# Talking-heads attention: the mixing stage laid out in 64x64 and 64x32 array tiles, with the attention turned by VectorE

## The chip, the cores and the metric

The kernel runs on one core of a Trainium2 chip. The metric is the device time of one execution in microseconds (us), as the median of several runs. A profile is one further execution, recorded by the hardware profiler. The engines are called PE (TensorE's matmuls), PEld (its weight loads), DVE (VectorE), ACT (ScalarE), POOL (GpSimd) and SP (SyncE, here only a queue that issues DMAs).

## What is computed

Two blocks follow each other. All data are fp32; the two feed-forward weights come in as 64-bit floats. With B = 8 batches, 12 heads, S = 448 positions and head size 64:

```python
scores = scale * q @ k.transpose            # (B, 12, S, S)
scores = einsum('bhij,hg->bgij', scores, w_pre)
attn = exp(scores - max(scores, axis=-1))
attn = attn / (sum(attn, axis=-1) + 1e-09)
attn = einsum('bhij,hg->bgij', attn, w_post)
x = (attn @ v)                              # to (B, S, 768)

u = x + real(fft(fft(x, axis=1), axis=2))
un = (u - mean(u)) / sqrt(var(u) + 1e-06)
out = u + maximum(un @ w_ch1, 0) @ w_ch2    # 768 -> 3072 -> 768
```

The heads are mixed with each other before the softmax (`w_pre`) and after it (`w_post`). That mixing runs over the head index at every pair of positions, so neither of the two products has a long inner dimension.

## The kernel before

`mix_phase` computes the attention, the Fourier mixing and the conversion of the feed-forward weights to fp32. `ffn_phase` then normalizes and runs the two products with the weights (matmuls L660 and L700). The change touches `mix_phase` alone.

**Tiles.** A tile is ten rows of queries of one batch with all 12 heads, so 120 partitions: `R = 10`, `KR = 120`, 45 tiles a batch, 360 in all. Twelve tiles make a group of up to 120 rows, four groups a batch. For each pair of heads q and k are loaded, transposed by PE against an identity (L221) and multiplied (`emit_qk`, L233): the two heads of a pair stand in partitions 0 to 63 and 64 to 127, so each of the two matmuls uses 64 rows of the array and 120 columns. The scores go from PSUM to the SBUF tile `Sb` (by ACT, L104, or by DVE, L106). A DMA gathers ten rows of twelve heads into `Kr`, with 120 partitions (`emit_gather`, L247).

**Per tile** there is one chain of steps:

1. `emit_premix` (L253): a block-diagonal 120x120 matrix of `w_pre` mixes the heads, 448 columns, into PSUM tile `mx` (two buffers).
2. `emit_max` (L260, DVE): the maximum of each row, negated, in `nmx`.
3. `emit_exp` (L269, ACT): the exponential into `PP` (four buffers), with the row sums in `den`.
4. `emit_scale` (L277, L279 on DVE, L282 on POOL): the reciprocal of the sum is multiplied into a copy of the `w_post` matrix, `kw2s`.
5. `emit_flip` (L290): four matmuls that take `PP` as weights, 112 columns at a time, so that the second mixing comes out already transposed in `fl`.
6. `emit_pav` (L104 or L106): `fl` is copied to `Pav`.

**Per group**, `emit_av` (L314) multiplies `Pav` with v, 48 matmuls of 64 columns twice, and POOL folds the result for the Fourier transform (L327 to L331). **Per batch**, `emit_z` (L344, seven chunks) and `emit_s2` (L368, one call per group) make the two Fourier products; DVE adds them to the rows (L376, L379).

**Weights.** `emit_convert` runs 96 times: POOL issues a load of 384 KB of 64-bit words (L396) into one of two buffers `raw`, DVE makes fp32 of it in seven instructions (L407 to L420) on `tmp` and `top`, and SP stores it (L422).

**Order.** A loop over tiles writes the steps of tiles s-1 to s+6 one after another and inserts the other work from one list, `fill`, sorted by due times. A scheduler then sets the order on every engine, PE included. `_Evac` chooses ACT or DVE for each copy out of PSUM by a running estimate of both engines' load.

## Time and profile before

| | us |
|---|---|
| median of 3 runs | 3179.82 (3176.68 to 3180.89) |
| the profiled execution | 3191.58, span of the core 3189.8 |
| `mix_phase`, to the first transpose of `ffn_phase` | 0 to 1591.5 |
| PE busy over the span | 3019.4 (95%) |
| PEld / DVE / ACT / POOL busy | 2167.1 / 1162.7 / 792.9 / 519.8 |
| granted TensorE clock, mean | 0.963 |

A profile's page begins with the busy time of each engine. A row of digits gives busy tenths of 40 equal slices of the span, here about 80 us each. `PEclk` is the share of full speed that TensorE was granted in each slice. A view by stage repeats these sums for chosen stretches, with the number of instructions in brackets. A row of the view by line gives line, engine, operation, output<-inputs, shapes and count, then the busy time, the mean of one in ns, and the engine's idle time just before, with what ended it. A shape such as 64*120 on a matmul is rows times columns of the array that it uses. An fp32 matmul shows as two weight loads and two matmul instructions. The length of a matmul instruction includes the time its last result needs to come out, so neighbours overlap. The chain of waits follows the work that ended last back in time and counts each moment once.

### The profile page before, as it was taken

To read this page: it belongs to the slowest core of one execution; us is meant where nothing else is said; L and a number is where in the kernel's file an instruction comes from. 1 tells how busy PE (TensorE), PEld (TensorE's weight loads), DVE (VectorE), ACT (ScalarE), POOL (GpSimd) and SP (SyncE) were. 2 spreads that over 40 slices of the span, in tenths; PEclk is the share of its full clock that TensorE was granted. 3 is DMA by queue.
4 is the path that set the end of the run, shared out by engine and by line. 5 is a ranking of instruction groups with operands and counts; after the bars stand their busy time and mean duration, and the time that the engine had idled before them with its cause. 6 is when DMAs were issued, how large, how long until landed. Compare 5 with 4: busy or idle time off the path is not lost.

```text
span 3189.8 us, 39781 instructions
## 1 busy us (share of the span) xinstructions
PE 3019.4 (95%) x14768; PEld 2167.1 (68%) x14768; DVE 1162.7 (36%) x2911; ACT 792.9 (25%) x1940; POOL 519.8 (16%) x869
## 2 busy tenths in 40 slices
PE   6888888899999999999999999999999999999998
PEld 3665565676767776766787686686686786776875
DVE  4667777533333333333653032122121221221220
ACT  3333333354545354544110010010010010110100
POOL 4242242141313131211110100100100100000000
PEclk8788988899999999999899999999999999999999
DMA  7566666453444444444875444444444444444433
GB/s 194 140 156 165 169 178 164 120 113 66 107 73 104 80 100 89 84 81 91 267 251 176 163 159 158 162 153 158 175 139 168 171 154 147 166 168 148 154 111 109
DMA packets 179798, 457.07 MB, mean 143 GB/s; under 512 B 19743, under 2 KB 122655, under 8 KB 167063
## 3 DMA queue, kind: packets, MB, share of 16 engines
q1 hardware_dynamic: 155063, 361.71, 40.2%
q0 software_dynamic: 24544, 92.82, 9.9%
q8 instruction: 119, 1.95, 0.2%
q14 instruction: 72, 0.59, 0.1%
HBM read 317.60 MB, written 59.77 MB: 118 GB/s over the span
## 4 chain that ended last, share of the span: by engine, by line
PE 66%; DMA 14%; issue 12%; DVE 5%; POOL 2%; SPq 1%; ACT 0%; POOLq 0%; DVEq 0%; ACTq 0%
PE ms L314 9%; PE psP L660 8%; PE fl L290 8%; PE psP L700 8%; PE mx L253 7%; DMA raw<-in_moe_w_ch_dram 6%; PE psR L700 6%; PE psR L660 5%; PE ms L233 4%; PE ms L368 4%; PE psQ L700 3%; DMA w1t<-w1f 3%; PE ms L344 2%; PE psQ L660 2%; DMA out_dram<-u 1%
## 5 line engine op out<-in xcount | busy, mean ns | idle before, releaser
L660 PE MATMUL psP<-ub,w1t 128*128 128x256 f32 x2016 | 465.8, 384 | 30.8 <-DVE mv L619 16.7
L290 PEld LDWEIGHTS fl<-kw2s,PP 120*112 120x112 f32 (+1 forms) x2880 | 349.5, 185 | 210.9 <-issue 117.2
L660 PEld LDWEIGHTS psP<-ub,w1t 128*128 128x128 f32 x2016 | 383.7, 192 | 98.0 <-DMA w1t<-w1f 25.8
L700 PE MATMUL psP<-w2t,h 128*128 128x384 f32 x1344 | 436.9, 486 | 0.0
L290 PE MATMUL fl<-kw2s,PP 120*112 120x120 f32 (+1 forms) x2880 | 389.7, 281 | 44.1 <-POOL kw2s L282 25.6
L253 PE MATMUL mx<-Kr,kw 120*120 120x448 f32 x720 | 350.2, 570 | 33.4 <-ACT PP L269 26.3
L700 PEld LDWEIGHTS psP<-w2t,h 128*128 128x128 f32 x1344 | 254.8, 190 | 173.1
L314 PEld LDWEIGHTS ms<-vn,Pav 112*120 112x120 f32 (+1 forms) x3072 | 341.0, 195 | 20.9 <-issue 16.9
L314 PE MATMUL ms<-vn,Pav 112*120 112x64 f32 (+1 forms) x3072 | 340.2, 278 | 7.6 <-issue 6.7
L269 ACT ACTIVATE PP<-mx,nmx 120x448 f32<-120x448 f32 x360 | 228.2, 634 | 470.7 <-DVE nmx L260 430.8
L260 DVE TENSOR_REDUCE nmx<-mx 120x1 f32<-120x448 f32 x360 | 222.3, 618 | 256.4 <-PE mx L253 254.3
L282 POOL TENSOR_SCALAR kw2s<-kw2g,rcp 120x120 f32<-120x120 f32 x360 | 148.2, 412 | 716.8 <-DVE rcp L279 648.2
L104 ACT COPY Pav<-fl 112x480 f32<-112x480 f32 x310 | 177.1, 571 | 273.0 <-PE ms L314 141.2
L660 PE MATMUL psR<-ub,w1t 128*128 128x256 f32 x1008 | 232.7, 380 | 0.9 <-DMA w1t<-w1s 0.7
L700 PE MATMUL psR<-w2t,h 128*128 128x384 f32 x672 | 220.0, 486 | 0.0
L637 POOL TENSOR_TENSOR ub<-ub 128x768 f32<-128x768 f32 x28 | 50.5, 1825 | 1038.2 <-ACT ub L632 1037.7
L233 PE MATMUL ms<-kT,qT 64*120 64x448 f32 (+1 forms) x768 | 206.9, 609 | 6.7 <-DVE Sb L106 5.0
L660 PEld LDWEIGHTS psR<-ub,w1t 128*128 128x128 f32 x1008 | 191.3, 190 | 28.2 <-DMA w1t<-w1s 2.6
L700 PEld LDWEIGHTS psR<-w2t,h 128*128 128x128 f32 x672 | 126.4, 190 | 84.1
L104 ACT COPY Sb<-ms 120x448 f32<-120x448 f32 (+1 forms) x324 | 161.2, 531 | 48.9 <-PE ms L233 48.7
L709 DVE TENSOR_TENSOR u<-u,psP 128x384 f32<-128x384 f32 x56 | 31.1, 555 | 341.6 <-PE psP L700 341.6
L632 ACT COPY ub<-psQ 128x384 f32<-128x384 f32 x56 | 24.8, 481 | 481.0 <-PE psQ L630 481.0
(86 smaller groups left out, 2758.4 us busy)
## 6 DMA issues: line engine op xcount, KB each, us to landing
Kr<-Sb SPq DMA_DIRECT2D x352, 210.0 KB
w2t<-w2s SPq DMA_DIRECT2D x56, 1152.0 KB
w2t<-w2f SPq DMA_DIRECT2D x42, 1152.0 KB
w1t<-w1s SPq DMA_DIRECT2D x72, 576.0 KB
raw<-in_moe_w_ch_dram POOLq DMA_DIRECT2D x96, 384.0 KB, 5.8
w1t<-w1f SPq DMA_DIRECT2D x84, 384.0 KB
w1t<-w1f SPq DMA_DIRECT2D x96, 192.0 KB
w1t<-w1s SPq DMA_DIRECT2D x72, 192.0 KB
```

The costliest lines, as they stand in the source:

```text
L104: self.nc.scalar.copy(out=out, in_=in_)
L233: nc.tensor.matmul(sp[:n, :S], st["qT", hp][x * D:(x + 1) * D, g["i0"]:g["i0"] + n], st["kT", hp][x * D:(x + 1) * D, :], start=True, stop= ...
L253: nc.tensor.matmul(mx[:m, :S], kw1[:m, :m], tiles[T]["Kr"][:m, :], start=True, stop=True)
L260: nc.vector.tensor_reduce(nmx[:m, :], tiles[T]["mx"][:m, :S], axis=AX.X, op=ALU.max, negate=True)
L269: nc.scalar.activation(PP[:m, :], tiles[T]["mx"][:m, :S], ACTF.Exp, bias=tiles[T]["nmx"][:m, :], accum_out=den[:m, :])
L282: nc.gpsimd.tensor_scalar(kw2s[:m, :], kw2g[:m, :], rcp[:m, :], 1.0, op0=ALU.mult, op1=ALU.mult)
L290: nc.tensor.matmul(fl[:PC, jc * KR:(jc + 1) * KR], tiles[T]["PP"][:m, jc * PC:(jc + 1) * PC], tiles[T]["kw2s"][:m, :], start=True, stop=True)
L314: nc.tensor.matmul(ps[:n, hl * D:(hl + 1) * D], g["Pav"][:, jc * NH + h, :n], st["v", h // 2][:, h % 2, jc * D:(jc + 1) * D], start=(jc == ...
L344: nc.tensor.matmul(ps[:w, :SH + 1], g["xf"][par][:n, d0:d0 + w], ts[:n, g["gi"], par, :], start=(g["gi"] == 0), stop=(g["gi"] == NG - 1))
L368: nc.tensor.matmul(ps[:n, :DH + 1], st["z", par, ch][:, i0:i0 + n], tab[:w, ch, :], start=(ch == 0), stop=(ch == len(chunks) - 1))
L660: nc.tensor.matmul(p, w[m][:, i, kc, :], ub[:, i, kc, :], start=opens and kc == 0, stop=kc == NK - 1, skip_group_check=True)
L700: nc.tensor.matmul(p, lhs[i][:, half * NQ + kf, x * P:(x + 1) * P], w[:, kf, :], start=opens and half == 0 and kf == 0, stop=half == 1 and ...
```

## The change

The mixing stage gets another layout. The names of the steps mostly stay.

- **Steps of 20 rows.** `R = 5` rows times 12 heads are 60 partitions. Four such sets make a step: two in partition halves, two in the free dimension (`x` and `z`). A block of 56 rows is three steps, a group of 112 rows six; a batch is 24 steps, all are 192. Some rows are computed twice.
- **Tiles of the array.** `emit_qk`, `emit_premix` and `emit_av` issue matmuls of 64 rows and 64 (or 60) columns, four places in the array; `emit_postmix`, which takes the place of `emit_flip`, issues 64x32, eight places. The transposes and the Fourier products keep the full array.
- **Second mixing.** `PP` is now the moving operand. POOL scales `PP` itself by the reciprocal (twice 448 columns). The result `po` is not transposed by the matmul; DVE turns it in 32x32 blocks (`emit_turn`) into `Pv`, which takes the place of the copies to `Pav`.
- **Attention times v** has v as weights (64x64) and 120 columns of `Pv` moving, 84 matmuls a group. Its result is transposed, so `emit_x` turns it back with six PE transposes per group.
- **Buffers.** `mx` and `po` have two PSUM banks and one buffer each, `PP` two buffers, `Kr` three; `ms` keeps four banks.
- **Gathers.** Four DMAs of 60 partitions per step.
- **Order.** Other work stands in three lists, by the form of array it uses ("tile", "full", "none"). PE keeps the order in which the code is written; the other engines are still ordered by the scheduler. Conversions are due every 1.9 steps instead of every 3.5 tiles.

The core of the diff:

```diff
-R = 10
-KR = NH * R
-GT = 12
+R = 5
+KR = R * NH
+NB = 56
+BS = 3
+GT = 2 * BS
+GR = 2 * NB
-WSTEP = 3.5
+WSTEP = 1.9
...
-        ca, cd = 190.0 + n * 0.833, 70.0 + n * 1.042
+        ca, cd = 165.0 + n * 0.833, 150.0 + n * 1.042
...
-    pkr = pool("pkr", 6)
-    ppp = pool("ppp", 4)
+    pkr = pool("pkr", 3)
+    ppp = pool("ppp", 2)
+    ppv = pool("ppv", 2)
-    pmx = pool("pmx", 2, space=bass.MemoryType.PSUM)
-    pfl = pool("pfl", 2, space=bass.MemoryType.PSUM)
+    pmx = pool("pmx", space=bass.MemoryType.PSUM)
+    ppo = pool("ppo", space=bass.MemoryType.PSUM)
...
+    def emit_qk(n, xx):
+        for y in range(2):
+            lo = r0 + MG * y
+            for x in range(2):
+                nc.tensor.matmul(
+                    pss[x][64 * y:64 * y + r0 + 64 - lo, :S],
+                    st["qT", xx][64 * x:64 * x + 64, y, lo:r0 + 64],
+                    st["kT", xx][64 * x:64 * x + 64, y, :],
+                    start=True, stop=True)
...
+    def emit_gather(T):
+        for z in range(2):
+            for x in range(2):
+                nc.sync.dma_start(out=Kr[64 * x:64 * x + KR, z, :], in_=...)
...
+    def emit_premix(T):
+        mx = pmx.tile([P, 2, 512], F32, name="mx", tag="mx")
+        for x in range(2):
+            for z in range(2):
+                nc.tensor.matmul(mx[64 * z:64 * z + 64, x, :S],
+                                 kw1[64 * x:64 * x + KR, :],
+                                 Kr[64 * x:64 * x + KR, z, :], start=True, stop=True)
...
+    def emit_exp(T):
+        for x in range(2):
+            nc.scalar.activation(PP[:, x, :], steps[T]["mx"][:, x, :S], ACTF.Exp, ...)
...
+    def emit_scale(T):
+        nc.gpsimd.tensor_scalar(den[:, :], den[:, :], 1e-9, None, op0=ALU.add)
+        nc.vector.reciprocal(out=rcp[:, :], in_=den[:, :])
+        for x in range(2):
+            nc.gpsimd.tensor_scalar(PP[:, x, :], PP[:, x, :], rcp[:, x:x + 1], 1.0,
+                                    op0=ALU.mult, op1=ALU.mult)
+
+    def emit_postmix(T):
+        for y in range(2):
+            for c in range(2):
+                for z in range(2):
+                    o = 64 * y + 32 * c
+                    nc.tensor.matmul(po[o:o + 32, z, :S],
+                                     kw2[64 * z:64 * z + KR, y, :],
+                                     PP[64 * z:64 * z + KR, :, c * HS:(c + 1) * HS],
+                                     start=True, stop=True)
+
+    def emit_turn(T):
+        nc.vector.transpose(
+            g["Pv"][:, T % GT, :].rearrange("p (z s) -> p z s", z=2),
+            steps[T]["po"][:, :, :S])
+
+    def emit_av(g):
+        for pr in range(3):
+            for jb in range(C7):
+                for x in range(2):
+                    for y in range(2):
+                        i = 2 * pr + x
+                        nc.tensor.matmul(
+                            pss[y][64 * x:64 * x + 64, pr * nu * R:(pr + 1) * nu * R],
+                            st["v"][64 * y:64 * y + 64, i, jb * D:(jb + 1) * D],
+                            _ap(Pv, ...), start=(jb == 0), stop=(jb == C7 - 1))
...
+    with tc.manual_schedule(engines={mybir.EngineType.PE}):
+        while s < TOT or any(fill.values()):
+            held = []
+            take("none", s)
+            if 0 <= s + LM < TOT:
+                emit_premix(s + LM)
+                emit_max(s + LM)
+                emit_exp(s + LM)
+            take("tile", s)
+            if 0 <= s < TOT:
+                emit_postmix(s)
+                emit_turn(s)
+            if 0 <= s + LM < TOT:
+                emit_scale(s + LM)
+            if 0 <= s + LG < TOT:
+                emit_gather(s + LG)
+            take("full", s)
+            for fn in held:
+                fn()
+            s += 1
```

On PE, in the middle of a batch, the order before was this (L290 second mixing, L253 first mixing, L233 scores, L314 attention times v; a row is a matmul, `x4` four of them):

```order
L314 MATMUL ms<-vn,Pav 120x64 x48
L290 MATMUL fl<-kw2s,PP 112x120 x4
L253 MATMUL mx<-Kr,kw_122 120x448
L233 MATMUL ms<-kT,qT 120x448 x2
L290 MATMUL fl<-kw2s,PP 112x120 x4
L253 MATMUL mx<-Kr,kw_122 120x448
```

The same place now (L294 first mixing, L268 scores, L361 attention times v, L333 second mixing, L394 transposes of `emit_x`):

```order
L294 MATMUL mx<-Kr,kw_131 64x448 x4
L268 MATMUL ms<-kT,qT 64x448 x2
L268 MATMUL ms<-kT,qT 60x448 x2
L361 MATMUL ms<-Pv,vv 64x120 x84
L333 MATMUL po<-PP,kw_132 32x448 x8
L294 MATMUL mx<-Kr,kw_131 64x448 x4
L268 MATMUL ms<-kT,qT 64x448 x2
L268 MATMUL ms<-kT,qT 60x448 x2
L333 MATMUL po<-PP,kw_132 32x448 x8
L394 MATMUL ms<-ident,XT 112x128 x6
```

Scores now stand in every step, attention times v stands between the first mixing of one step and the second mixing of the step two before, and full-array work stands behind the second mixing.

On ACT, in the second half of the stage, the order before mixed single exponentials (L269) with copies (L104):

```order
L104 COPY Pav<-fl 112x48x10
L269 ACTIVATE PP,den<-mx,nmx 120x448
L104 COPY Pav<-fl 112x48x10
L269 ACTIVATE PP,den<-mx,nmx 120x448
L104 COPY kT<-ms 128x448
L104 COPY Sb<-ms 120x448
L104 COPY qT<-ms 128x448
L269 ACTIVATE PP,den<-mx,nmx 120x448
```

It is now, with the exponentials at L310 and the copies at L118 and L381:

```order
L310 ACTIVATE PP,den<-mx,nmx 128x448 x2
L381 COPY XT<-ms 128x3x60 x4
L118 COPY Sb<-ms 124x448 x2
L310 ACTIVATE PP,den<-mx,nmx 128x448 x2
L118 COPY Sb<-ms 124x448 x2
L310 ACTIVATE PP,den<-mx,nmx 128x448 x2
L118 COPY X<-ms 112x384 x2
```

The copies of `Pav` are gone, and nearly every copy that is left stands on ACT between two pairs of exponentials; DVE keeps 15 copies, all at the start.

On DVE, beside the conversions, the order before was (L407 to L420 the conversion, L260 maximum, L277 and L279 reciprocal):

```order
L413 SCALAR_TENSOR_TENSOR top<-raw_4973,top 128x384
L416 TENSOR_SCALAR tmp<-top 128x384
L418 SCALAR_TENSOR_TENSOR tmp<-raw_4973,tmp 128x384
L106 COPY Pav<-fl 112x48x10
L106 COPY X<-ms 88x384
L420 TENSOR_TENSOR top<-top,tmp 128x384
L260 TENSOR_REDUCE nmx<-mx 120x1
L407 TENSOR_SCALAR tmp<-raw_5117 128x384
```

and now (L468 to L481 the conversion, L301 maximum, L344 turn, L320 reciprocal):

```order
L344 STREAM_TRANSPOSE Pv<-po 128x896
L481 TENSOR_TENSOR top<-top,tmp 128x384
L320 RECIPROCAL rcp<-den 128x2
L474 SCALAR_TENSOR_TENSOR top<-raw_1267,top 128x384
L477 TENSOR_SCALAR tmp<-top 128x384
L479 SCALAR_TENSOR_TENSOR tmp<-raw_1267,tmp 128x384
L301 TENSOR_REDUCE nmx<-mx 128x2
L481 TENSOR_TENSOR top<-top,tmp 128x384
```

The conversion's instructions are the same seven; between them stand a maximum and a turn of twice the columns. The last conversion stood behind the 110th of 360 maxima and stands behind the 56th of 192.

More of the change, by code (lines that the diff above doesn't have):

```diff
@@ L21 @@
 NHP = NH // 2
[L24 to L34 removed]
+R = 5
+KR = R * NH
+RS = 12
+NB = 56
+BS = 3
+GT = 2 * BS
+GR = 2 * NB
+NG = S // GR
+GS = NG * GT
+TOT = B * GS
+C7 = 7
+HS = S // 2
+MG = 4
+WQ = S + 2 * MG
 SH = S // 2
@@ L305, in emit_av, with emit_tables @@
[L305 to L324 removed]
+    def emit_tables():
+        for t, n in ((ts, "ts"), (tce, "tc"), (tdo, "td")):
+            nc.sync.dma_start(out=t, in_=cn[n].ap())
+        return []
@@ L462, in mix_phase @@
[L462 to L495 removed]
+        return [done]
@@ new lines, in mix_phase, with take @@
+    due("none", 2, emit_tables)
+    for x, cut in enumerate(weights):
+        due("none", x * WSTEP, lambda cut=cut: emit_convert(*cut))
+    for v_ in fill.values():
+        v_.sort(key=lambda e: (e[0], e[1]))
+    def take(kind, s):
+        evs = []
+        while fill[kind] and fill[kind][0][0] <= s:
+            evs = fill[kind].pop(0)[2]()
+            if kind == "none":
+                held.extend(evs)
+                continue
+            for fn in evs:
+                fn()
+    s = int(min(v_[0][0] for v_ in fill.values()))
```

482 lines of the change are left out of this document (213 added, 269 removed).

## Prediction

> **What bounds the kernel now.** I read the page first, then the busy time by stage, then the stages one by one. Times are in microseconds unless marked ns.
>
> ```profile
> span 3189.8 us, 39781 instructions
> DVE  4667777533333333333653032122121221221220
> PEclk8788988899999999999899999999999999999999
> ```
>
> The DVE row splits the program. VectorE is busy in the first eight slices and half idle after them, and the granted TensorE clock is below full in just those slices and near slice 20. The busy time by stage puts numbers on this (columns: stretch, its length, busy PE, PEld, DVE, ACT, POOL with instruction counts, granted clock, DMA share, GB/s).
>
> ```profile
> 100.00:617.00 517.00, 434.26 (x2309) 303.80 (x2309) 355.70 (x960) 166.60 (x405) 157.29 (x264) 0.85 0.63 158
> 617.00:1500.00 883.00, 882.41 (x5704) 628.32 (x5703) 313.16 (x905) 428.49 (x1035) 227.39 (x441) 1.00 0.45 89
> 1500.00:1591.50 91.50, 79.24 (x429) 62.09 (x428) 53.77 (x133) 15.86 (x39) 15.34 (x24) 0.85 0.78 248
> 1591.50:3189.80 1598.30, 1555.23 (x6049) 1135.07 (x6047) 389.57 (x774) 150.72 (x392) 74.27 (x64) 1.00 0.46 160
> ```
>
> The mixing stage is the first 1591.5; the feed-forward stage behind it, 1598.3, is not touched. Until 617 the weight conversions run, and neither PE (84%) nor DVE (69%) is full. From 617 to 1500 PE is full at full clock: this clean stretch is bound by TensorE. How many tiles each holds is counted by their row maxima:
>
> ```profile
> 100.00:617.00 517.00, 57.83 (x94) 0.85 0.63 158
> 617.00:1500.00 883.00, 147.82 (x239) 1.00 0.45 89
> ```
>
> So a tile of ten rows costs 883/239 = 3.69 in the clean stretch and 517/94 = 5.5 beside the conversions. What TensorE does per tile stands in the chain of waits (start, length, work, matmul instructions; an fp32 matmul is two instructions):
>
> ```profile
> 703.27 7.50 PE ms L314 x96
> ...
> 711.64 0.75 PE mx L253 x2
> 712.39 0.95 PE ms L233 x4
> 713.34 1.00 PE fl L290 x8
> ...
> 715.10 3.05 PE ms L344 x16
> ...
> 736.84 4.73 PE ms L368 x14
> ```
>
> The first mixing (L253) is 0.75 for two passes over 448 columns, the second (L290) 0.8 to 1.0, attention times v (L314) 7.5 per group of heads and rows, one Fourier chunk (eight instructions of L344) 1.52, the last Fourier product (L368) 4.73.
>
> What bounds the conversion stretch shows in who waits for whom, and in the conversions' own DVE work:
>
> ```profile
> DVE tmp L407 <- DMA raw<-in_moe_w_ch_dram: 121.7, 55, 5.6
> POOL raw L396 <- DVE tmp L418: 74.4, 35, 5.2
> ...
> L413 DVE SCALAR_TENSOR_TENSOR top<-raw,top 128x384 uint32<-128x384 uint32 x86 | 50.7, 589 | 1.8
> ...
> 100.00:617.00 517.00, 217.69 (x515) 0.85 0.63 158
> ...
> raw<-in_moe_w_ch_dram POOLq DMA_DIRECT2D x96, 384.0 KB, 5.8
> ```
>
> There are 86 conversions in those 517, one per 6.0. Each keeps DVE busy for (217.7 + 50.7)/86 = 3.1 (the instructions on tmp, and L413). The two raw buffers form a ring: the load lands 5.8 after its issue, DVE works the piece off with other work between, POOL may then issue the next load. DVE waits for the load, POOL for DVE. That ring, not TensorE, sets 6.0 here.
>
> **The change, part by part.** A step now mixes 20 rows; a batch is 24 steps, all 192. In the new order the last conversion stands behind the 56th row maximum of 192, where it stood behind the 110th of 360: the same 30% of the work.
>
> *Conversion stretch.* Seven DVE instructions per piece, two raw buffers and the 96 loads are unchanged. DVE's other work per piece stays alike: 56/96 steps with a maximum and a turn. The row for one maximum over 448 columns is
>
> ```profile
> L260 DVE TENSOR_REDUCE nmx<-mx 120x1 f32<-120x448 f32 x352 | 217.3, 618 | 254.2 <-PE mx L253 252.1
> L282 POOL TENSOR_SCALAR kw2s<-kw2g,rcp 120x120 f32<-120x120 f32 x352 | 143.8, 409 | 700.5 <-DVE rcp L279 631.9 <-PE mx L253 44.1 <-PE fl L290 12.4
> ```
>
> so over 896 columns 1.24 each, 2.5 a step, 1.5 a piece: lower bound for the stretch 96 x (3.1 + 1.5) + 28 of start = 470. The upper bound is a ring of 7.5 a piece, from POOL: it now scales the exponentials themselves, twice 448 columns per step where it scaled 120 (409 ns; 0.4 to 1.5 each by columns), and the raw loads queue behind that: 96 x 7.5 + 28 = 750. I take the measured ring, 96 x 6.0 + 28 = 605, because loads, buffers and DVE work per piece are the same; before it was 617.
>
> *A step of the clean stretch.* First whether array tiles run side by side. The scores already use half the array's rows:
>
> ```profile
> L233 PE MATMUL ms<-kT,qT 64*120 64x448 f32 x576 | 158.1, 617 | 6.7 <-DVE Sb L106 5.0 <-DVE rcp L279 1.1 <-ACT Sb L104 0.5
> ...
> 1003.74 1.01 PE L233 MATMUL ms<-kT,qT 64*120 64x448 f32 x4
> 1004.68 1.07 PE L290 MATMUL fl<-kw2s,PP 120*112 120x120 f32 x8
> 1005.60 0.92 PE L253 MATMUL mx<-Kr,kw 120*120 120x448 f32 x2
> ```
>
> Four instructions of 617 ns end within 1.01, so two row tiles do run at once, in 0.75 of streaming. The remaining 0.95 - 0.75 = 0.2 of the chain's piece is what going into and out of a tiled form costs. Column tiles appear nowhere in this trace. I take it that they overlap like row tiles, since each has its own weights and its own output partitions. The Trainium skill (TensorEngine Tiling (Array Packing), Key Properties) says that tiles operate independently, row and column alike; no run here shows the column half of that. By the row alone, only two would overlap, which is a rival below.
>
> Then: first mixing 0.75 (four 64x64 tiles, for 20 rows), scores 0.75, change to 64x32 tiles 0.15, second mixing 0.75. L253's 0.92 on the timeline against 0.75 in the chain says that a result is there 0.17 after streaming. Now a wait that did not exist: PP has two buffers, so the exponential of step k waits for the second mixing of step k-2, which stands behind the scores on PE; and mx has one, so the next first mixing waits for that exponential. Behind the exponential on ACT stand the copies of the scores and of the Fourier chunks.
>
> ```profile
> L269 ACT ACTIVATE PP<-mx,nmx 120x448 f32<-120x448 f32 x352 | 223.2, 634 | 457.6 <-DVE nmx L260 417.9 <-DVE rcp L277 30.9 <-DVE rcp L279 8.4
> ...
> L269 ACT ACTIVATION_READ_ACCUMULATOR PP<-mx,nmx 120x1 f32 x352 | 68.3, 194 | 0.0
> ...
> L104 ACT COPY Sb<-ms 120x448 f32<-120x448 f32 x231 | 116.2, 534 | 46.0 <-PE ms L233 45.8
> ```
>
> Two exponentials are 2 x (0.634 + 0.194) = 1.66. The ring is 0.75 + 0.75 + 0.15 + 0.75 + 0.17 + 1.66 + 0.15 = 4.4 a step, 105.6 a batch. Before, 24 steps' rows were 45 x 3.69 = 166 with everything in it. The maximum (1.24) lies beside scores and second mixing; the two copies of scores (1.07) beside the next first mixing. The turn (1.24, bounded by one and two maxima) must be done before the next second mixing, 3.6 later; if DVE were late there, the ring would grow by its lateness. POOL's scaling (up to 3 with the reciprocal) has 6 until its mixing. Gathers are now four a step on SP's queue:
>
> ```profile
> L247 SPq DMA_DIRECT2D Kr<-Sb x104: 702/812/4547, 115.7 to 646.3; - x104
> ```
>
> 4 x 0.81 = 3.2 of 4.4, two steps ahead of use: covered.
>
> *What is added to the ring.* Attention times v sits inside it, four times a batch: 84 matmuls, 168 instruction pairs. Four at once and streamed (120 columns at 0.75/896 = 0.84 ns, so 100 ns for each of 42 rounds of four pairs) they take 4.2; at the 7.50/96 = 78 ns per pair of L314 they take 13.1. That row's pairs load 88 columns of weights, here 64, and on four tiles instead of one, so it is nearer to the lower end: 6.0, 24 a batch. Fourier chunks and products fit into PE's idle time under the exponentials, about 1.65 a step. Two chunks in a step (3.05) exceed it by 1.4, three times; a product (about 4.6) by 2.95, four times; doubled transposes by 0.7: 16.7 a batch.
>
> *Clock.* PE now idles 2.0 in a step without such work. What idling does:
>
> ```profile
> 440.35 0.60 PE L221 MATMUL ms<-ident,rawk 112*128 112x112 f32 x4 [2.28 <-ACT kT L104]
> ...
> 437.50:440.90 3.40, 1.12 (x10) 0.99 0.74 230
> 440.90:444.30 3.40, 3.40 (x11) 0.50 0.90 188
> ```
>
> After 2.28 of idling the clock was 0.50 for the next 3.4. With idling of 2.0 in 6 of 24 steps I charge 6 a batch. The Trainium skill (TensorE: Matmul & The Clock Gate, Why this matters for your kernels) asks only that gaps stay under about 3 us; the trace disagrees, with a halved clock after 2.28. By the page the 6 would go and the sum would be 34 lower.
>
> *End of the stage.* Last attention times v, chunks and products ran from 1546.97 to 1591.62:
>
> ```profile
> 1546.97 14.31 PE L314 MATMUL ms<-vn,Pav 112*88 112x64 f32 x96 [0.84 <-DVE Pav L106]
> ...
> 1591.62 0.82 PE L630 MATMUL psQ<-ident,un 128*128 128x128 f32 x6
> ```
>
> I keep 45, plus 6 for the feed-forward stage's weight sums that already slowed the last 11 tiles (47 for what costs 41 at 3.69).
>
> **Sum.** A batch is 105.6 + 24 + 16.7 + 6 = 152.3, and 136 steps are 5.67 batches: 863. Mixing stage 605 + 863 + 51 = 1519 against 1591.5, 72.5 less. The profiled execution took 3191.58 (span 3189.8) and the median of three runs is 3179.82; the difference is taken off the median: **3107**. Its own range is 3020 to 3170 (attention times v 4.2 to 8; a ring of 4.1 to 4.6 with stalls).
>
> **Rivals.**
> - *Both unknowns go well*: conversions at DVE's bound of 470 (-135) and attention times v at 4.2 (-1.8 x 4 x 5.67 = -41): 2931. For it: DVE's waits for raw loads are 121.7 of the stretch. Against: POOL has more in front of those loads.
> - *The clock stays halved* in the 13 light steps of a batch: their 2.25 of streaming and the changes of form take twice as long, 2.3 more each, 30 in all, and attention times v 8.4 for 6.0, 10 in all, less the 6 charged: 34 x 5.67 = +193, 3300. It decides once streaming falls to about a third of 3.4 (1.12 of 3.40 above); a plain step streams 2.25 of 4.4 with 2.0 of idling in one piece, so some windows of 3.4 hold only 1.4 of it. The conversion stretch (clock 0.85) speaks for it, the Fourier work in the gaps against.
> - *TensorE takes pairs no faster than 78 ns*: attention times v 13.1, +7.1 x 4 x 5.67 = +161, 3268. Nothing in this trace is faster than 78 ns per pair.
> - *Raw loads held up by POOL*: 7.5 a piece, +144, 3251. POOL waits in order for reciprocals, and a raw load behind it waits too.
> - *Column tiles take turns*: first mixing and scores +0.75 each, second mixing +2.25, attention times v 8.4: 3.75 x 24 + 2.4 x 4 = 99.6 a batch, +565, 3672. The change then would not do what it says. Nothing here speaks for it but the lack of a row.
>
> **How the numbers follow.** Forecast 0.45, all well 0.13, clock 0.14, pairs 0.09, raw loads 0.12, column tiles 0.07. About 0.2% (6) can be told from no change. Faster: nearly all of the forecast and the first rival, 0.56; the same: 0.04; slower: 0.40. The range 2925 to 3305 reaches from the first rival to the clock's and leaves out column tiles and the tails.
>
> **What would show it.** In the new trace: the L294 group at 0.75 per step for eight instructions (right) or 1.5 (column tiles take turns); the length of the 168 pairs of L361, 4.2 to 13.1; the exponential L310 released by PE's second mixing and premixing released by ACT; the last conversion near 605; granted clock from there above 0.9; steps of 6.3 behind it. I am wrong if the conversions end before 520 or after 700, if a step of the clean stretch takes over 7.4 (136 steps as long as before), or if ACT or DVE is full there.

## The result and the profile after

The changed kernel takes **3001.77 us** (median of four runs, 2998.21 to 3005.09), the kernel before 3178.25 beside it: a ratio of 0.9448 (95% interval 0.9429 to 0.9467), 176 us less where 73 were forecast. The direction was right and the time lies in the range, but the gain is more than twice the forecast. All times are in microseconds. The profiled execution of the kernel before was 13 above its median, so the two profiles lie 191 apart instead of 176.

The page of the changed kernel: its span, VectorE's row and the granted clock.

```profile
span 2999.2 us, 47325 instructions
...
DVE  4878888644444444457430320320320320320220
...
PEclk8687887999999999988999999999999999999999
```

The busy part of VectorE's row, and the low clock with it, ends one slice earlier than before. The same stretches as in the prediction, now cut at the last conversion (553.9), the last maximum (1346.0) and the feed-forward stage's first transpose (1401.9); the columns are length, PE, PEld, DVE, ACT, POOL, granted clock, DMA share, GB/s:

```profile
100.00:553.90 453.90, 278.62 (x3148) 128.40 (x3156) 378.97 (x765) 144.02 (x382) 187.01 (x316) 0.79 0.62 180
553.90:1346.00 792.10, 680.32 (x9148) 345.33 (x9132) 367.82 (x515) 405.51 (x1075) 330.91 (x622) 0.99 0.37 116
1346.00:1401.90 55.90, 41.79 (x319) 28.60 (x320) 38.44 (x87) 7.31 (x24) 10.13 (x16) 0.85 0.96 342
1401.90:2999.20 1597.30, 1558.61 (x6049) 1135.85 (x6047) 389.07 (x760) 150.84 (x392) 73.46 (x62) 0.99 0.45 158
```

The feed-forward stage is as long as before (1597.3 and 1598.3), so the gain is the mixing stage's: 1401.9 instead of 1591.5 in the two profiles. TensorE is no longer full in the clean stretch (680 of 792, 86%), yet its clock is 0.99. VectorE's maxima, counted in the same stretches, give the steps:

```profile
100.00:553.90 453.90, 50.80 (x48) 0.79 0.62 180
553.90:1346.00 792.10, 147.92 (x136) 0.99 0.37 116
```

136 steps in 792.1 are 5.82 each; 6.35 was forecast. One plain step on the timeline (start, length, work, instructions):

```profile
936.08 0.98 PE L294 MATMUL mx<-Kr,kw 60*64 60x448 f32 x8 [1.64 <-ACT PP L310]
...
936.88 0.93 PE L268 MATMUL ms<-kT,qT 64*64 64x448 f32 x8
...
937.20 1.09 DVE L301 TENSOR_REDUCE nmx<-mx 128x2 f32<-128x896 f32 x1 [0.68 <-PE mx L294]
...
937.74 0.98 PE L333 MATMUL po<-PP,kw 60*32 60x448 f32 x16
937.86 0.97 ACT L118 COPY Sb<-ms 124x448 f32<-124x448 f32 x2 [1.84 <-PE ms L268]
938.83 1.12 DVE L344 STREAM_TRANSPOSE Pv<-po 128x896 f32<-128x896 f32 x1 [0.54 <-PE po L333]
938.97 0.63 ACT L310 ACTIVATE PP<-mx,nmx 128x448 f32<-128x448 f32 x1
...
940.36 0.98 PE L294 MATMUL mx<-Kr,kw 60*64 60x448 f32 x8 [1.64 <-ACT PP L310]
941.16 4.60 PE L361 MATMUL ms<-Pv,vv 64*64 64x120 f32 x168
```

Eight instructions of the first mixing, eight of the scores and sixteen of the second mixing each take just under 1.0 with the last result's way out: all tiles of a piece run at once. The maximum is there at 938.29, but the exponential starts at 938.97, behind the second mixing (to 938.72) and the score copies on ACT (to 938.83). The next first mixing waits for it, and TensorE idles 1.64. That is the forecast ring, but for the place of the two copies: the forecast had them behind the exponential, and here they stand ahead of it and end last. Attention times v, 168 pairs, takes 4.60.

Whole steps, one view with a batch, a plain step, one with attention times v, one with Fourier chunks and one with a product:

```profile
819.04:957.38 138.34, 119.49 (x1618) 60.68 (x1618) 63.63 (x88) 73.73 (x194) 62.14 (x116) 1.00 0.38 116
923.39:927.59 4.20, 2.65 (x33) 0.69 (x33) 2.37 (x3) 3.00 (x8) 3.51 (x6) 1.00 0.35 131
940.36:948.98 8.62, 7.07 (x200) 5.12 (x200) 2.37 (x3) 3.09 (x10) 2.85 (x5) 1.00 0.24 62
824.84:830.62 5.78, 5.78 (x49) 3.20 (x48) 2.37 (x3) 3.48 (x10) 1.37 (x4) 1.00 0.30 112
853.12:860.42 7.30, 7.30 (x47) 3.16 (x47) 3.68 (x7) 2.95 (x8) 3.58 (x6) 1.00 0.31 106
```

For the conversion stretch, VectorE's wait for raw pieces, POOL's for VectorE, and the landing of a raw load:

```profile
POOL raw L457 <- DVE tmp L479: 82.8, 31, 5.2
...
DVE tmp L468 <- DMA raw<-in_moe_w_ch_dram: 57.9, 50, 7.3
...
raw<-in_moe_w_ch_dram POOLq DMA_DIRECT2D x96, 384.0 KB, 4.0
```

VectorE is busy 83% there (379 of 454; 69% before) and waits half as long for loads, which land 4.0 after their issue instead of 5.8, although the forecast took the loads as unchanged. Why they land sooner was the first thing to find out.

### The profile page after: what moved, and what is told of

It is laid out like the page before. It is cut to its first block, busy times and chain, and to the rows that moved or that the text cites. A ratio compares the mean times of both kernels' runs of the same rounds, so it can differ in the third digit from the quotient of the medians.

```text
span 2999.2 us, 47325 instructions
## 1 busy us (share of the span) xinstructions
PE 2610.3 (87%) x18992; PEld 1655.9 (55%) x18992; DVE 1228.7 (41%) x2242; ACT 734.3 (24%) x1931; POOL 649.5 (22%) x1101
## 4 chain that ended last, share of the span: by engine, by line
PE 41%; issue 11%; DMA 7%; ACT 2%; DVE 1%; SPq 1%; POOL 1%; ACTq 0%; POOLq 0%; DVEq 0%
PE psP L715 9%; PE psP L755 8%; PE psR L755 6%; PE psR L715 5%; PE psQ L755 3%; DMA w1t<-w1f 3%; PE psQ L715 2%; DMA out_dram<-u 2%; PE mx L294 1%; PE ms L436 1%; DMA w2t<-w2f 1%; DMA u<-u_scr 1%; ACT PP L310 1%; PE ms L268 1%; PE ms L361 1%
## 5 line engine op out<-in xcount | busy, mean ns | idle before, releaser
L294 PE MATMUL mx<-Kr,kw 60*64 60x448 f32 x1536 | 209.0, 611 | 211.4 <-ACT PP L310 206.6
L310 ACT ACTIVATE PP<-mx,nmx 128x448 f32<-128x448 f32 x384 | 240.2, 630 | 225.2 <-DVE nmx L301 194.1
L333 PE MATMUL po<-PP,kw 60*32 60x448 f32 x3072 | 209.8, 605 | 95.4 <-DVE Pv L344 71.9
L323 POOL TENSOR_SCALAR PP<-PP,rcp 128x448 f32<-128x448 f32 x384 | 252.8, 667 | 128.5 <-DVE rcp L320 123.8
L344 DVE STREAM_TRANSPOSE Pv<-po 128x896 f32<-128x896 f32 x192 | 213.6, 1112 | 157.1 <-PE po L333 157.1
L118 ACT COPY Sb<-ms 124x448 f32<-124x448 f32 x375 | 182.8, 541 | 308.3 <-PE ms L268 282.8
L301 DVE TENSOR_REDUCE nmx<-mx 128x2 f32<-128x896 f32 x192 | 208.6, 1086 | 113.1 <-PE mx L294 113.1
L294 PEld LDWEIGHTS mx<-Kr,kw 60*64 60x64 f32 x1536 | 43.1, 140 | 321.9 <-ACT PP L310 298.8
L268 PE MATMUL ms<-kT,qT 64*64 64x448 f32 (+1 forms) x1536 | 203.3, 589 | 4.6 <-DVE X L447 3.3
L333 PEld LDWEIGHTS po<-PP,kw 60*32 60x32 f32 x3072 | 36.8, 109 | 237.0 <-issue 169.3
L361 PEld LDWEIGHTS ms<-Pv,vv 64*64 64x64 f32 x5376 | 154.4, 139 | 21.6 <-issue 17.7
L361 PE MATMUL ms<-Pv,vv 64*64 64x120 f32 x5376 | 157.5, 273 | 3.6 <-DVE Pv L344 1.9
```

The source lines that it names most:

```text
L118: self.nc.scalar.copy(out=out, in_=in_)
L268: nc.tensor.matmul(pss[x][64 * y:64 * y + r0 + 64 - lo, :S], st["qT", xx][64 * x:64 * x + 64, y, lo:r0 + 64], st["kT", xx][64 * x:64 * x + ...
L294: nc.tensor.matmul(mx[64 * z:64 * z + 64, x, :S], kw1[64 * x:64 * x + KR, :], Kr[64 * x:64 * x + KR, z, :], start=True, stop=True)
L301: nc.vector.tensor_reduce(nmx[:, :], steps[T]["mx"][:, :, :S], axis=AX.X, op=ALU.max, negate=True)
L310: nc.scalar.activation(PP[:, x, :], steps[T]["mx"][:, x, :S], ACTF.Exp, bias=steps[T]["nmx"][:, x:x + 1], accum_out=den[:, x:x + 1])
L323: nc.gpsimd.tensor_scalar(PP[:, x, :], PP[:, x, :], rcp[:, x:x + 1], 1.0, op0=ALU.mult, op1=ALU.mult)
```

## Experiments

Theory: the changed kernel's clean stretch is the ring first mixing, scores, second mixing, exponential; it is short because tiles run side by side, and it keeps the clock. The conversion stretch is a ring of loads that the change shortened by something other than array tiles. Ratios are against the kernel before, run on the same chip, each with its interval; the changed kernel stands at 0.9448.

**Where the gathers read.** Before, a tile's ten rows are ten adjacent partitions of `Sb`; now they lie twelve apart. First the changed kernel with adjacent rows:

```diff
-                p0 = MG + 4 * (T % BS) + 2 * z + x
+                p0 = MG + 10 * (4 * (T % BS) + 2 * z + x)
...
-                    in_=_ap(Sb, p0 * row, [[RS * row, 2 * R], [S, 6], [1, S]]))
+                    in_=_ap(Sb, p0 * row, [[row, 2 * R], [S, 6], [1, S]]))
```

> Each gather of scores reads ten adjacent partitions of Sb, as before the change, instead of ten partitions that lie twelve apart; sizes and counts of the transfers are the same (which query rows are mixed together changes, so the output's rows come out in another order). Source theory for the 52 us that the conversion stretch was shorter than forecast: transfers from adjacent partitions take longer, so with them raw loads land 5 us or more after their issue instead of 3.9, the last conversion moves from 553 to 590-605 and the whole to about 3040; the clean stretch does not notice. Rival, the smaller gathers (105 KB to 60 partitions instead of 210 KB to 120) or the other traffic made the difference: no change within 6 us, raw loads land at 3.9 as now.

Measured: 3024.92, ratio 0.9539 (0.9514 to 0.9563). The last conversion came at 568, not 590 to 605, and the raw loads still landed in 4.1:

```profile
raw<-in_moe_w_ch_dram POOLq DMA_DIRECT2D x96, 384.0 KB, 4.1
```

Then the kernel before with rows twelve apart:

```diff
-        nc.sync.dma_start(out=Kr[:n * NH, :], in_=g["Sb"][r0:r0 + n, :, :])
+        src = g["Sb"][r0:r0 + n, :, :]
+        if g["n"] == GT:
+            row = _row(g["Sb"])
+            src = _ap(g["Sb"], (T - g["f"]) * row, [[GT * row, R], [S, NH], [1, S]])
+        nc.sync.dma_start(out=Kr[:n * NH, :], in_=src)
```

> The kernel before, with one edit: the gather of a tile's scores reads ten partitions of Sb that lie twelve apart instead of ten adjacent ones, in groups of twelve tiles (which query rows are mixed together changes, so the output's rows come out in another order). Source theory: raw loads land about 4 to 4.5 us after their issue instead of 5.7, the conversion stretch of the kernel before falls from 617 to about 570, the clean stretch stays full of TensorE work at 3.69 us a tile; about 3130 in all. Rival, the size of the gathers or other traffic sets the landing: 5.7 stays and the time is that of the kernel before within 6 us.

Measured: 3093.28, ratio 0.9754 (0.9734 to 0.9775); the last conversion at 516 instead of 617. The explicit strides could have changed the scheduler's order as well. So the same form was run over the adjacent rows (`r0 * row, [[row, R], ...`):

> The kernel before with its gathers written with the same explicit strides as in the run with spread rows, but over the ten adjacent partitions of the original, so that the data moved is that of the kernel before. Every engine's instructions stand in exactly the order of the run with spread rows (which differs from the kernel before's order on every engine, so that run changed two things at once). Source theory: order alone gives little, the time is that of the kernel before within 20 (about 3160 to 3190), the last conversion near 617, raw loads land about 5.7 after issue, and the 79 us of the run with spread rows are the partitions'. Rival, the planner's other order made it faster: about 3093, last conversion near 516, raw loads at 4.

Measured: 3177.82, ratio 0.9994 (0.9981 to 1.0008), last conversion at 609.8. The expectation says that the order of these two runs differs from that of the kernel before; the traces, in which tiles carry no buffer numbers, show the same sequence of operations, tiles and shapes on every engine in all three. So the partitions alone are worth 79: 3093.28 is 79.5 below the kernel before beside it, and 3177.82 is 0.4 below. The two stretches of the run with adjacent rows and the landing of its raw loads, then those of the one with spread rows:

```profile
100.00:609.80 509.80, 428.12 (x2333) 297.23 (x2333) 358.86 (x966) 167.85 (x409) 158.12 (x266) 0.86 0.65 162
609.80:1533.90 924.10, 913.15 (x5897) 652.11 (x5895) 331.46 (x957) 438.77 (x1060) 233.61 (x453) 0.99 0.46 94
...
raw<-in_moe_w_ch_dram POOLq DMA_DIRECT2D x96, 384.0 KB, 5.5
```

```profile
100.00:516.20 416.20, 367.27 (x2198) 251.75 (x2199) 346.31 (x934) 161.99 (x396) 154.82 (x258) 0.95 0.66 191
516.20:1446.60 930.40, 922.66 (x5900) 661.77 (x5898) 331.18 (x957) 438.59 (x1060) 234.91 (x453) 0.98 0.31 93
...
raw<-in_moe_w_ch_dram POOLq DMA_DIRECT2D x96, 384.0 KB, 4.0
```

The gain is all in the conversion stretch; the clean one, full of TensorE work, is 6 longer. The queue that holds the gathers, in the clean stretch of these two runs (packets, MB, share of 16 engines' time):

```profile
q1 hardware_dynamic: 38531, 66.59, 38.8%
```

```profile
q1 hardware_dynamic: 38516, 66.55, 22.9%
```

A packet takes 16 x 924.1 x 0.388 / 38531 = 149 ns from adjacent rows and 16 x 930.4 x 0.229 / 38516 = 88 ns from spread ones. The same in the changed kernel's clean stretch, as it is and with adjacent rows (792.1 and 800.4 long):

```profile
q1 hardware_dynamic: 43144, 71.18, 26.1%
```

```profile
q1 hardware_dynamic: 43150, 71.19, 39.9%
```

That is 77 and 118 ns. The Trainium skill (SBUF — State Buffer, Door 1: The DMA port swizzle) says that four neighbouring partitions share one of 16 ports and that a transfer's rate goes by the ports it reaches; counted by its table, the ten adjacent rows of these gathers reach three, ten rows twelve apart reach ten. The four numbers agree in direction; no run varies the ports in another way.

So the source theory holds in the kernel before, where spreading shortens the conversion stretch by 94 and lets raw loads land in 4.0 instead of 5.5. In the changed kernel it is worth 23 (3024.92 - 3001.77; 29 by the two ratios), of which 14 lie in the conversion stretch and 8 in the clean one, and raw loads land in 4.1 even with adjacent rows. So there the rows are not what lets them land sooner than 5.8. It could be the size of the gathers. Cutting the old gather in two was meant to show it:

```diff
+        h = n // 2
+        for a, z in ((0, h), (h, n)):
+            nc.sync.dma_start(out=Kr[a * NH:z * NH, :],
+                              in_=g["Sb"][r0 + a:r0 + z, :, :])
```

> The kernel before, each gather of a tile's scores cut into two transfers of five rows (60 partitions, 105 KB) instead of one of ten rows (120 partitions, 210 KB); they still read adjacent partitions and bring the same data. Size theory for what the spread rows leave open of the 52 us: smaller transfers disturb the raw loads less, these land at 5 us or sooner instead of 5.8, the last conversion comes at 590 or sooner instead of 617, the whole about 25 to 35 less. Source theory: only where the rows lie counts, the last conversion stays at 617 within 10 and the time within 10 of the kernel before, or is up to 30 longer for the added issues.

Measured: 3278.91, ratio 1.0325 (1.0292 to 1.0358), last conversion at 681. Neither theory said so. The raw loads landed in 5.5, hardly sooner than 5.8. On the gathers' queue this is the clean stretch, 939.4 long:

```profile
q1 hardware_dynamic: 36948, 64.05, 27.3%
```

A packet took 16 x 939.4 x 0.273 / 36948 = 111 ns there, less than the 118 of the changed kernel with adjacent rows, whose raw loads land in 4.1. So neither gathers of 105 KB nor shorter packets were enough here for an early landing. But the order of instructions changed on every engine in this run, so size and order aren't told apart. By the Trainium skill (DMA: Bandwidth & Descriptors, Why a DMA increments its semaphore by 16 and not by 1) a transfer gets as many engines, up to 16, as divide the slowest dimension of both its sides: by that rule, ten for ten rows and five for the five of a half. That would speak against cutting by rows; no run here shows the engines.

**What else sets the conversion stretch.** A third raw buffer (`bufs=3` on `raw64`):

> The raw weight pieces of the conversions get three buffers instead of two; nothing else is edited. Ring theory of the conversion stretch (load, VectorE, next load): VectorE's 58 us of waiting for raw pieces between 100 and 553 go, the last conversion moves from 553 to about 500, the whole falls by about 50 to 2950. Rival, VectorE (busy 378 of those 453) and the maxima and turns that it must wait for between two pieces set the stretch by now: the last conversion stays within 10 of 553 and the time within 10 of 3002.

Measured: 2991.69, ratio 0.9404 (0.9372 to 0.9436), whose interval meets the changed kernel's. VectorE's wait for raw pieces fell from 57.9 to 25.7. The last conversion came at 519, but behind the 52nd maximum instead of the 56th, and those four steps had to be run afterwards (4 x 5.82 = 23 of the 35). So the stretch gained about 12 where 50 were expected: the load's landing hardly sets the pace any more, and the rival is nearer. Without conversions (a transfer of zeros in each piece's place):

> The conversion of the weights is left out: no raw loads and no VectorE work for it; each piece's place in the scratch is written with zeros from one tile by a transfer of the same size, so the feed-forward stage runs on zeros and the output is not the reference's. Theory that the conversions only stretch the steps beside them: all 192 steps run at the 5.81 us of the clean stretch, mixing stage 44 + 192 x 5.81 + 57 = 1217 instead of 1402, the whole 2817. Rival, the first steps are also slowed by a cold start of loads and by the low clock (0.79 there) that lasts without conversions too: the stage stays above 1300.

Measured: 2833.04, ratio 0.8904 (0.8877 to 0.8931), 16 above what was expected. The mixing stage ends at 1233, its 192 maxima lie between 75.6 and 1169.9, 5.70 a step: the pace of the clean stretch from the start. The conversions cost the changed kernel 169.

**Whether column tiles run side by side.** Both heads of a pair in the same columns:

```diff
-                            pss[y][64 * x:64 * x + 64, pr * nu * R:(pr + 1) * nu * R],
+                            pss[y][:64, pr * nu * R:(pr + 1) * nu * R],
...
-                            start=(jb == 0), stop=(jb == C7 - 1),
+                            start=(jb + x == 0), stop=(jb + x == C7),
```

> Attention times v issues its 84 matmuls with the same shapes, but both heads of a pair go to the array's first 64 columns, so that only the two row tiles can run side by side (the two heads are summed into one result, and the other half of XT is set to zero by GpSimd: the output is not the reference's). Theory that column tiles overlap: a group's 168 instruction pairs take about 8.8 us instead of 4.60, 22 groups of the clean stretch +4.2 each, 93 us, and up to 40 more beside the conversions: 3095 to 3135. Rival, the pairs are limited by their issue at 27 ns a pair, and overlap of columns gives nothing: 4.6 as now, time within 15 of 3002.

Measured: 3134.29, ratio 0.9856 (0.9829 to 0.9882), 133 above the changed kernel.

```profile
1110.51 8.92 PE L361 MATMUL ms<-Pv,vv 64*64 64x120 f32 x168
```

The same 168 pairs take 8.92 instead of 4.60. Columns overlap, and 4.60 is 27 ns a pair (4.60/168). Whether issue would allow less than that isn't shown. The Trainium skill (TensorEngine Tiling (Array Packing), Key Properties) calls tiles independent; this pair of runs agrees, 4.60 against 8.92.

**The ring.** First a third PP buffer (`pool("ppp", 3)`):

> Exponentials PP get three buffers instead of two; nothing else is edited. Ring theory: in the clean stretch the exponential of step k waits for the second mixing of step k-2, which stands behind the scores or attention times v on TensorE, and the copies of the scores get ahead of it on ACT meanwhile. With a third buffer it waits for its maximum only: a plain step falls from 4.20 us to about 3.6 (first mixing 0.98, maximum 1.1, exponentials 1.4, hand-overs), a step with attention times v from 8.62 to about 6.8 (its TensorE work alone), steps with Fourier work stay. 13 x 0.6 + 4 x 1.8 = 15 a batch, 5.5 batches: about 80 us less, 2920. Rival, the one buffer of the mixed scores mx and TensorE's own work set the step, so PP's wait only covers them: 0 to 20 us less. The conversion stretch stays near 553 by both.

Measured: 2965.44, ratio 0.9348 (0.9324 to 0.9373): the fastest version of this study, 32 to 36 below the changed kernel, but under half of what was expected. A step with attention times v fell to 7.00, near the expected 6.8, but only three of a batch's four: the fourth holds Fourier work too and was full already (8.72 in both kernels). A plain one fell to 3.92 instead of 3.6:

```profile
771.78 0.98 PE L294 MATMUL mx<-Kr,kw 60*64 60x448 f32 x8 [1.31 <-ACT PP L310]
...
772.15 1.10 DVE L344 STREAM_TRANSPOSE Pv<-po 128x896 f32<-128x896 f32 x1
...
773.17 1.05 DVE L301 TENSOR_REDUCE nmx<-mx 128x2 f32<-128x896 f32 x1
...
774.31 0.63 ACT L310 ACTIVATE PP<-mx,nmx 128x448 f32<-128x448 f32 x1 [1.72 <-DVE nmx L301]
```

The exponential now waits for its maximum only, as expected, but VectorE turns the step before until 773.2, and the maximum, whose data are there at 772.8, waits for that. A new wait stands where the old one was. And once a batch, at the first Fourier chunk, a step now begins with a wait for its gather (the first mixing, then the whole step):

```profile
794.87 2.19 PE L294 MATMUL mx<-Kr,kw 60*64 60x448 f32 x5 [1.72 <-DMA Kr<-Sb]
...
794.87:803.36 8.49, 8.49 (x49) 4.31 (x49) 3.45 (x5) 2.84 (x9) 3.41 (x7) 0.80 0.34 129
```

It takes 8.49 at a clock of 0.80, where the changed kernel takes 5.80 at full clock. In all, 128 steps behind the conversions took 5.56 each instead of 5.82, about 34 less. The conversions ended level: 598 behind the 64th maximum, where 553.9 + 8 x 5.82 = 600 would be level.

Now the second mixing ahead of the other work:

```diff
+            if 0 <= s < TOT:
+                emit_postmix(s)
+                emit_turn(s)
             take("tile", s)
-            if 0 <= s < TOT:
-                emit_postmix(s)
-                emit_turn(s)
```

> On TensorE the second mixing of a step is put ahead of the step's scores or attention times v instead of behind them; buffers unchanged. Ring theory: the exponential that waits for that second mixing is free at once, and scores and attention times v run beneath maximum and exponential: plain step 3.6 to 3.7 instead of 4.20, step with attention times v about 6.8 instead of 8.62, steps with Fourier work unchanged, about 80 us less, 2920, as with a third PP buffer. Rival, the second mixing is itself late (POOL's scaling or VectorE's turn of the step before releases it): then it holds up scores and attention times v behind it, and the time stays or grows by up to 50 us.

Measured: 2993.51, ratio 0.9437 (0.9419 to 0.9454), not told from the changed kernel. Plain steps took 3.73 and those with attention times v 7.03, as the ring theory said, and yet the gain is absent. Part of it is lost where a batch's first chunk follows a step that waits for its gather (a step before it, the step, and a step behind it; then its first mixing on the timeline):

```profile
676.68:682.43 5.75, 2.81 (x32) 0.61 (x33) 2.45 (x4) 3.76 (x10) 3.87 (x8) 0.98 0.91 210
682.43:692.84 10.41, 9.82 (x49) 3.88 (x49) 2.37 (x3) 2.79 (x8) 2.59 (x5) 0.68 0.29 104
692.84:698.78 5.94, 5.94 (x49) 3.10 (x48) 2.28 (x3) 3.37 (x10) 1.46 (x3) 1.00 0.35 128
```

```profile
682.43 1.72 PE L294 MATMUL mx<-Kr,kw 60*64 60x448 f32 x2 [2.94 <-DMA Kr<-Sb]
```

After 2.94 of idling the clock is 0.68 over the next step, which takes 10.4 instead of 5.9; this comes back in every batch. The conversions also ended later: 647 behind the 70th maximum, where 553.9 + 14 x 5.82 = 635 would be level.

**How near the clock's edge is.** One more exponential in each step:

```diff
-        for x in range(2):
+        for x in (0, 0, 1):
             nc.scalar.activation(PP[:, x, :], steps[T]["mx"][:, x, :S], ACTF.Exp,
```

> The exponential of each step's first half is computed twice, one more ACT instruction of 0.63 us in every step; TensorE's work is unchanged and it idles about 2.2 us instead of 1.6 in a step without Fourier work. Ring without a clock effect: the 17 of 24 steps that wait for the exponentials grow by 0.63, 5.5 batches: 59 us, and up to 30 more beside the conversions: 3060 to 3090, granted clock of the clean stretch 0.99 as now. Rival, the clock cliff: a plain step then streams under 40% of 3.4 us, the clock halves as it did in the kernel before after 2.28 of idling, each of the 13 plain steps loses about 2 more: 3200 to 3250, granted clock of the clean stretch 0.8 or less.

Measured: 3199.05, ratio 1.0054 (1.0027 to 1.0081): 197 more for one more exponential a step, 0.5% above the kernel before. From the last conversion to the last maximum:

```profile
547.00:1537.00 990.00, 794.32 (x9554) 382.67 (x9554) 383.68 (x534) 518.89 (x1408) 341.07 (x643) 0.89 0.31 97
```

```profile
1036.93 0.98 PE L294 MATMUL mx<-Kr,kw 60*64 60x448 f32 x8 [2.33 <-ACT PP L310]
...
1037.74 1.60 PE L268 MATMUL ms<-kT,qT 64*64 64x448 f32 x8
...
1039.27 1.74 PE L333 MATMUL po<-PP,kw 60*32 60x448 f32 x16
```

After 2.33 of idling the scores and the second mixing take 1.60 and 1.74 instead of 0.93 and 0.98. To be sure that it is the clock, TensorE was given idle-time work on top:

```diff
+            if 0 <= s < TOT and not 4 <= s % GS < 12:
+                ps = ms_tile()
+                for n in range(8):
+                    nc.tensor.matmul(ps[:, :P], ident[:, :], ident[:, :],
+                                     start=True, stop=True)
```

> As the kernel with the third exponential (3199 us, granted clock 0.89 from 612 to 1550), and in each step without Fourier chunks or products TensorE also multiplies the identity by itself, eight matmuls of 128 columns behind the second mixing, whose result nobody reads: about 0.9 us of streaming in time that TensorE idles anyway. Clock theory: TensorE streams enough to keep its clock, plain steps fall from 6.1-6.6 to about 4.9, granted clock of the clean stretch 0.97 or more, the whole 3060 to 3110, although TensorE has more to do. Rival, the third exponential costs its 190 us by the ring (later scaling, turn and copies) and not by the clock: the time stays at 3199 or grows by up to 80 from the added work.

Measured: 3106.82, ratio 0.9774 (0.9749 to 0.98).

```profile
540.00:1448.00 908.00, 882.99 (x11088) 530.50 (x11082) 385.87 (x535) 531.53 (x1416) 342.97 (x648) 1.00 0.34 107
```

More work, 92 less time, clock 1.00: at least 92 of the 197 are the clock's. The same work without the third exponential:

> The changed kernel with the same idle-time matmuls of the identity (eight of 128 columns behind the second mixing in each step without Fourier chunks or products, result unread) and no third exponential. If the clock costs nothing in the clean stretch any more, its plain steps stay at 4.20 to 4.3. In the conversion stretch the granted clock rises from 0.79 to 0.9 or more; if TensorE's slower clock there held the ring up, the last conversion moves from 553 to 520-540 and the whole falls by 10 to 30; if VectorE sets that stretch, nothing changes but up to 15 us more for the added work.

Measured: 3071.02, ratio 0.9664 (0.9636 to 0.9691), 69 more than the changed kernel. It came out worse than the "up to 15": where the clock is full anyway, the added work only lengthens steps (plain 4.56 for 4.20). In the conversion stretch the clock rose from 0.79 to 0.83 and the last conversion, at 546 behind the 52nd maximum, came no earlier for its place (553.9 - 4 x 5.82 = 531 would be level). What a full clock would bring there, the run doesn't show.

## Why the prediction was right in direction and short in size

| term | forecast | measured |
|---|---|---|
| conversion stretch | 605 | 553.9 |
| 136 steps of the clean stretch | 863 | 792.1 |
| end of the stage | 51 | 55.9 |
| mixing stage | 1519 | 1401.9 |

Most of the mechanism was right: array tiles run side by side in rows and columns, the step is a ring of the pieces that were written, Fourier work fills TensorE's idle time, the feed-forward stage is unchanged. One step was wrong in its reason, the conversion stretch, which was carried over as measured (605, and it took 553.9). In the clean stretch (863, and it took 792.1) two terms were too large: attention times v, 24 a batch for 17.7, and the clock, 6 a batch for 0. Nearly all errors go one way, so they add up.

*Conversion stretch, 51 too long.* The step that failed is "I take the measured ring, 96 x 6.0 + 28 = 605, because loads, buffers and DVE work per piece are the same". The raw loads are the same, but not what runs beside them: the gathers' source rows moved from ten adjacent partitions to ten that lie twelve apart, which the diff shows as `RS`. In the kernel before this alone takes the last conversion from 610 to 516, with the raw loads' landing from 5.5 to 4.0. In the changed kernel it explains little: with adjacent rows its raw loads land in 4.1. Seen from the kernel before, spreading gives 94 and the other edits take 38 back (516 to 554); seen from the changed kernel, spreading gives 14 (568 to 554) and the rest of the change 42 (610 to 568). The parts don't add up, and what makes up the 42 was not separated, so the cause of the larger part stays open. Candidates are VectorE's larger share, smaller gathers (though the cut gathers above didn't bring an early landing) and the loads of q and k, whose form changed too: they landed 6.1 after their issue and now take 4.0 and 3.9. The 5.8 of the raw load's landing stood in the quoted row as a cause, and I asked what POOL would add to it, not what it consisted of.

*Clean stretch, 71 too long.* By batch: ring 24 x 4.20 = 100.8 for 105.6; attention times v 4 x (8.62 - 4.20) = 17.7 for 24; clock 0 for 6. Fourier work and doubled transposes are what the quoted batch leaves, 138.34 - 100.8 - 17.7 = 19.8 for 16.7: in the quoted rows a chunk step is 1.6 and a product step 3.1 longer than a plain one. That makes 138 for 152.3; with the steps at its two edges the stretch comes to 5.82 x 24 = 139.8 a batch, 12.5 less than forecast, 5.67 times. The slot of attention times v was the largest miss: 4.42 where I took 6.0, between bounds of 4.2 and 13.1, of which the lower was nearly right. A limit of 78 ns a pair doesn't show with tiles of 64x64.

*Clock.* I charged 34 for idling of 2.0; hardly anything was lost, and TensorE idles 1.64 here at a clock of 0.99. By the page's rule (the Trainium skill, TensorE: Matmul & The Clock Gate, Why this matters for your kernels: gaps under about 3 us) nothing was to be charged, which came out right for this kernel. But with gaps of 2.33 the clock fell, and in the run with a third PP buffer it fell behind one of 1.72 (above), so a bound of 3 is too high. The length of one gap isn't the whole rule either, since the run without conversions kept its full clock behind 1.92 (the step's first mixing, then the 3.41 from its start):

```profile
1120.41 0.98 PE L294 MATMUL mx<-Kr,kw 60*64 60x448 f32 x8 [1.92 <-ACT PP L310]
...
1120.41:1123.82 3.41, 3.41 (x88) 2.51 (x92) 1.26 (x2) 0.97 (x2) 1.46 (x3) 1.00 0.20 70
```

In steps that repeat, 1.64 kept the clock and 2.33 did not; what decides in between was not separated. The rival "the clock stays halved" (3300) was only 0.7 of idling away: one more exponential a step gave 3199.

*Rivals.* Columns that take turns: the 8.92 of the run on one column half shows what that would have been for attention times v. Raw loads held up by POOL: no, a piece took 5.5 ((553.9 - 28)/96), not 7.5. "Both go well" (2931) was nearly right for attention times v, not for conversions, which stay 84 above VectorE's bound of 470. Of the signs that the forecast named, one did not show: the exponential starts behind the score copies on ACT, not at the end of the second mixing.

*End.* 55.9 for 51; the DMA share is 0.96 in it.

## What to carry to other kernels

When a change moves where data lie, read its transfers as new ones, even if sizes and counts agree: ask from which partitions each transfer reads. When TensorE stops being full, work out the longest gap in a step and how far it is from the gaps at which the clock fell in the trace at hand; past that edge, 0.7 us more of idling in a step went with 197 us here, at least 92 of them the clock's. And when a wait is removed, name the next one from the timeline: the third PP buffer gave 32 to 36 of 80, because VectorE's order came next, and once a batch a gather.

## What the runs showed of the hardware

- On the queue that holds the gathers a packet took 149 ns on average with sources in ten adjacent partitions and 88 ns with sources twelve apart (118 and 77 in the changed kernel's form), at the same count and size. In the first pair of runs raw loads landed 5.5 and 4.0 after their issue, in the second 4.1 and 4.0.
- Four 64x64 tiles took 168 instruction pairs of 120 columns in 4.60, 27 ns a pair; on one column half 8.92.
- TensorE kept its full clock with gaps of 1.64 in steps of 4.2, ran its next pieces at little over half speed after gaps of 2.33, and kept it again when matmuls that nobody reads shortened the gap. Single gaps of 1.72 (clock 0.80 in the step behind it) and 1.92 (clock 1.00 behind it) show that the length of one gap alone doesn't settle it.
